# Where the outer rows of Wq are loaded from, and the row sizes of two sets of zero fills, in a decode step with its gradients

## The chip, the cores and the metric

One NeuronCore of a Trainium2 chip runs the whole kernel. The metric is device time in microseconds (us), the median of the runs shown. Engines are called as the profile calls them: PE (matmuls), DVE, ACT, POOL (GpSimd) and SP; the core has 16 DMA engines that all queues share.

## The reference

One token (batch 1, width 448) goes through an attention block with a sliding window over a key and value cache, and then through a bilinear feed-forward block. The outputs are the result and the gradients of x, both caches and all weights.

```python
def _A_ref(x, k_cache, v_cache, wq, wo):          # x normalised before
    W = 4096                                      # window of the 32768 positions
    q = heads(x @ wq)                             # 16 heads of 256
    k, v = last W positions of each cache, 8 kv heads, each for two q heads
    p = softmax(q k^T * Dh ** -0.5)
    return (p v) @ wo
h  = x + _A_ref(layernorm(x), ...)
h2 = h + ((n @ w_gate) * (n @ w_up)) @ w_down     # n = layernorm(h)
_out, _vjp = jax.vjp(f, x, k_cache, v_cache, wq, wo, w_gate, w_up, w_down)
return (_out, *_vjp(grad_out))
```

Only the last 4096 of 32768 positions of a cache get a gradient. The gradient of the other 28672 positions is zero, for 8 heads and two caches, and must be written all the same: 16 regions of 14 MB in `out_2` and `out_3`.

## The kernel before, in words

Wq (448 x 4096, 28 KB per partition when laid over 128 partitions) lives in the tile `zeros`, but not fully. Partitions 0 to 31 and 96 to 127 hold rows of Wq. In partitions 32 to 95 every fourth one (32, 36, ..., 92) is zeroed, 16 partitions in all, and is the source of the zero fills; the three between hold Wq rows. The Wq rows that the zero partitions displace are kept in part of the tile `Mt`, called `odd`.

The start, in the order of the code:

- L58 and L60: ACT's queue loads x and grad_out.
- L69: SP's queue loads Wq rows 0 to 31 in one DMA (32 partitions x 28 KB). L70: ACT's queue loads rows 96 to 127 in one DMA.
- L80 (`load_odd`, L76 to L78): SP's queue loads the displaced rows in four DMAs of 128 KB, packets of 4 KB.
- L81 to L86: DVE and ACT zero partitions 32 to 95 of `zeros` and parts of `odd`. DVE clears columns 0 to 8191 of partitions 32 to 63, then of 64 to 95 (L82), then the remaining columns of 32 to 63 (L83); ACT does the remaining columns of 64 to 95 (L84).
- L87 and L88: ACT's queue loads the Wq rows of partitions 33 to 95 that are not zero rows, three DMAs of 16 rows.
- L99 to L103: SP's queue gets the 15 full zero fills, each one region of 14 MB, 16 source partitions, in rows of 16 KB (`ZW`, 8192 elements), or of 28 KB (`NW`) for the regions in `LONG`. The first needs the memsets of L82.
- L116 to L118: SP's queue gets a part of the sixteenth region. `deal(eng, e0, k, n, f)` fills from `k` zero partitions starting with number `e0`, `n` rows of `f` elements from each; `deal_all` does it from all 16. The rest of that region is left to GpSimd, in two laps (`deal_rest`, L120 to L131): lap 0 after the output h2 (L566 to L568), lap 1 after the last gradients (L803 and L804).
- L178 to L183: GpSimd's queue loads the windows K0, V0, K1, V1 and V2 (2 MB each).

Then the forward pass runs over the 8 kv heads: scores, softmax, moments (`scores`, `softmax`, `moments`, L377 to L440), with GpSimd loading further windows as buffers come free (L460 to L470), then Wo, the feed-forward block and its gradients (to L595), then the gradient of the attention (from L597). In its last stage (L766 to L802) PE makes the outer products for the gradients of K and V, ACT and DVE copy them from PSUM to slots of the tile `BIG` (`evac`, L297), and GpSimd's queue writes a pair of slots per head (L801 and L802). In between GpSimd also writes the weights' gradients (`outer`, L644 to L652); the first of these (L715) write `out_7` from the slots that the gradients of the first head want next.

Each engine's instructions run in their program order, its DMAs too, and the scheduler adds semaphore waits. SP issues nothing but DMAs: its list of fills is a background stream that the DMA engines serve beside the loads and stores on GpSimd's queue. A zero fill's rows are written from the partitions given; `deal` thus sets how many bytes go from which zero partition.

```python
def fill(eng, flat, rows, n, f):
    p = len(range(128)[rows])
    eng.dma_start(out=flat.rearrange("(p n f) -> p n f", p=p, f=f), in_=zeros[rows, 0:f].unsqueeze(1).to_broadcast([p, n, f]))
```

Of the kernel before, what the change touches and what calls it, by code (L numbers as in the profile page):

```python
# [17 lines left out]
G = 8  # L18
# [9 lines left out]
HQ = H * Dh // 2  # L28
HF = F // 2
ZW = 8192  # L30
NW = NI * HQ
FL = (Sk - W) * Dh // 16

# [9 lines left out]
def kernel(  # L43
# [3 lines left out]
    V_, S_, P_ = nc.vector, nc.scalar, nc.tensor  # L47
    FILL = nc.sync
    IO = nc.gpsimd
# [12 lines left out]
    def flat_rows(w):  # L62
        return w.rearrange("a b -> (a b)").rearrange("(p x) -> p x", p=128)

    zeros = const.tile([128, NW], bf16)
    one = const.tile([128, 1], f32)
    V_.memset(one[:], 1.0)
    wq_rows = flat_rows(A_wq)
    FILL.dma_start(out=zeros[0:32, :], in_=wq_rows[0:32, :])  # L69
    S_.dma_start(out=zeros[96:128, :], in_=wq_rows[96:128, :])  # L70
    Mt = const.tile([128, G, 2, 2 * Dh], bf16)
    late = Mt[:].rearrange("p g f c -> p (g f c)")
    odd = late[:, 2 * HQ:4 * HQ]
    wq_odd = A_wq.rearrange("a b -> (a b)")[32 * NW:96 * NW].rearrange("(e h k c) -> e h k c", h=NI, k=4, c=HQ)

    def load_odd(eng):  # L76
        for k in range(4):
            eng.dma_start(out=odd[32 + k:96:4, :].rearrange("p (h c) -> p h c", h=2), in_=wq_odd[:, 0:2, k, :])  # L78

    load_odd(FILL)  # L80
    for p in (32, 64):  # L81
        V_.memset(zeros[p:p + 32, 0:ZW], 0.0)  # L82
    V_.memset(zeros[32:64, ZW:NW], 0.0)  # L83
    S_.activation(out=zeros[64:96, ZW:NW], in_=one[64:96, 0:1].to_broadcast([32, NW - ZW]), func=ACT.Copy, scale=0.0)  # L84
    for p in (0, 96):
# [4 lines left out]
    def region(o, g):  # L90
        return o[0, g, 0:Sk - W, :].rearrange("s d -> (s d)")
# [5 lines that stand above are left out]
    ALL = slice(32, 93, 4)  # L97
    LONG = range(5, 10)
    for g in range(G):  # L99
        for k, o in enumerate((out_2, out_3)):  # L100
            if (g, k) != (G - 1, 1):
                f = NW if 2 * g + k in LONG else ZW
                fill(FILL, region(o, g), ALL, FL // f, f)  # L103
    last = region(out_3, G - 1)
    used = [0]

    def deal(eng, e0, k, n, f=ZW):
        p0 = 32 + 4 * e0
        fill(eng, last[used[0]:used[0] + k * n * f], slice(p0, p0 + 4 * k - 3, 4), n, f)
        used[0] += k * n * f  # L110

    def deal_all(n, f):
        fill(FILL, last[used[0]:used[0] + 16 * n * f], ALL, n, f)
        used[0] += 16 * n * f

    deal(FILL, 0, 3, 14)  # L116
    deal_all(24, ZW)
    deal_all(8, 1224)  # L118

    def deal_rest(lap):  # L120
        if lap == 0:
            deal(IO, 0, 4, 24)
            deal(IO, 4, 3, 6)
            deal(IO, 7, 2, 38)
            deal(IO, 9, 7, 15)
        else:
            deal(IO, 0, 5, 2, 512)
            deal(IO, 5, 2, 25)
            deal(IO, 7, 2, 2, 512)
            deal(IO, 9, 7, 15)  # L130
            assert used[0] == 896 * ZW  # L131

# [423 lines left out]
    for n, (s, m0, m1) in enumerate(CH):  # L556
# [3 lines left out]
        for m in range(m0, m1):  # L560
            c = NI * s + m
# [5 lines left out]
    with tc.issue_after(h2_out.ins):  # L567
        deal_rest(0)  # L568
# [46 lines left out]
    for h in range(H):  # L615
        for dk in range(2):
            for hf in range(2):
                c0 = (h % 2) * Dh + dk * 128
                g = h // 2
# [150 lines left out]
    for s, g in enumerate(SEQ):  # L770
# [3 lines left out]
        for t in range(T):  # L774
            d_ps = bps.tile([128, 2, Dh], f32, tag="d2", bufs=4)
            k, a = t // 8, t % 8
# [26 lines left out]
    with tc.issue_after(tail.ins):  # L803
        deal_rest(1)  # L804
# [31 lines left out]
```

## Time and profile before

| what | value |
|---|---|
| median of 3 runs | 784.82 us (784.43 to 785.53) |
| the profiled execution | 784.74 us, of it 782.9 in the profile's span |
| PE, DVE, ACT, POOL busy | 60%, 52%, 21%, 5% of the span |
| bytes moved by DMA | 329.70 MB (SP's queue 228.94, GpSimd's 97.77) |
| HBM | 48.40 MB read, 280.59 MB written |
| first Wq DMA, SP (L69) | issued at 0.75, 896 KB, 6.9 us to landing |
| first Wq DMA, ACT (L70) | issued at 1.57, 896 KB, 13.0 us to landing |
| K0 (L157) | issued at 1.29, 2048 KB, 17.8 us to landing |
| lap 0 of GpSimd's fills | issued from 372.89, 1536, 288, 1216 and 1680 KB, landing 47.4, 54.1, 101.9 and 111.4 us after issue |
| last gradients' DMAs (L802), lap 1 | issued at 739.76 and 740.83 |

How to read it: the profile is one execution, its times count from the span's start. A view gives, for 40 equal slices or for stretches that one names, how busy each engine was, the mean busy share of the 16 DMA engines, and the GB/s that they moved. Another lists each queue's packets, MB and share of the DMA engines' time: q1 is SP's, q10 ACT's, q0 GpSimd's. A landing is counted from the issue, so it includes the time in the queue.

### The profile page before, as it was taken

To read this page: it belongs to the slowest core of one execution; us is meant where nothing else is said; L and a number is where in the kernel's file an instruction comes from. 1 tells how busy PE (TensorE), PEld (TensorE's weight loads), DVE (VectorE), ACT (ScalarE), POOL (GpSimd) and SP (SyncE) were. 2 spreads that over 40 slices of the span, in tenths; PEclk is the share of its full clock that TensorE was granted. 3 is DMA by queue.
4 is the path that set the end of the run, shared out by engine and by line. 5 is a ranking of instruction groups with operands and counts; after the bars stand their busy time and mean duration, and the time that the engine had idled before them with its cause. 6 is when DMAs were issued, how large, how long until landed. Compare 5 with 4: busy or idle time off the path is not lost.

```text
span 782.9 us, 11090 instructions
## 1 busy us (share of the span) xinstructions
PE 471.6 (60%) x4506; PEld 260.9 (33%) x4506; DVE 403.7 (52%) x1190; ACT 162.0 (21%) x270; POOL 42.3 (5%) x86
## 2 busy tenths in 40 slices
PE   0769999989897540303223377089978678862600
PEld 0656555555564220301113243034423233320300
DVE  7436776666676310202566543066656456589500
ACT  4022212211220000000210033044533334421300
POOL 2000000000000000000100100000000000000200
PEclk9999999999999765555555555555555555555555
DMA  9999999999999999999999999999999999999996
GB/s 285 425 427 425 427 429 426 427 428 424 432 424 425 438 426 434 432 433 434 427 426 437 426 423 420 431 430 433 429 425 429 429 433 428 428 431 429 430 431 270
DMA packets 23188, 329.70 MB, mean 421 GB/s; under 512 B 3149, under 2 KB 3151, under 8 KB 4486
## 3 DMA queue, kind: packets, MB, share of 16 engines
q1 hardware_dynamic: 12589, 228.94, 68.6%
q0 software_dynamic: 10400, 97.77, 29.8%
q10 hardware_dynamic: 148, 2.30, 0.9%
q8 instruction: 35, 0.57, 0.3%
q14 instruction: 16, 0.12, 0.0%
HBM read 48.40 MB, written 280.59 MB: 420 GB/s over the span
## 4 chain that ended last, share of the span: by engine, by line
PE 36%; DMA 31%; DVE 14%; issue 7%; ACT 4%; another core or an unknown queue 3%; POOL 1%; POOLq 0%; DVEq 0%; ACTq 0%
DMA BIG<-in_A_k_cache_dram 10%; DMA out_dram<-BIG 9%; DMA BIG<-in_B_w_down_dram 8%; PE d_ps L777 8%; PE tr L363 8%; PE MT L420 8%; ACT BIG L299 3%; DMA BIG<-in_A_wo_dram 3%; DVE BIG L602 3%; DVE BIG L663 2%; DMA BIG<-in_A_v_cache_dram 2%; DVE BIG L591 2%; DVE BIG L301 2%; PE dp L368 2%
## 5 line engine op out<-in xcount | busy, mean ns | idle before, releaser
L777 PE MATMUL d_ps<-BIG 32*128 32x512 bf16 x256 | 121.1, 599 | 65.1 <-ACT BIG L299 47.7
L420 PE MATMUL MT<-BIG 128*128 128x512 bf16 x512 | 142.2, 391 | 4.1 <-DMA BIG<-in_A_v_cache_dram 4.1
L416 DVE TENSOR_SCALAR BIG<-BIG,pf 128x256 bf16<-128x256 bf16 x512 | 111.6, 281 | 34.3 <-PE MT L420 32.1
L363 PE MATMUL tr<-ident_bf,BIG 128*128 128x128 bf16 x1024 | 113.3, 269 | 20.7 <-DVE doW L602 12.6
L299 ACT CAST BIG<-d_ps 128x512 bf16<-128x512 f32 x156 | 88.4, 587 | 180.2 <-PE d_ps L777 129.5
L363 PEld LDWEIGHTS <-BIG 128*128 128x128 bf16 x1024 | 81.6, 121 | 65.1 <-issue 57.0
L301 DVE COPY BIG<-tr 128x1024 bf16<-128x1024 bf16 x92 | 63.3, 688 | 53.2 <-PE tr L363 50.3
L301 DVE CAST BIG<-d_ps 128x512 bf16<-128x512 f32 x100 | 68.0, 684 | 39.4 <-DMA out_dram<-BIG 33.4
L299 ACT COPY BIG<-tr 128x1024 bf16<-128x1024 bf16 x36 | 36.4, 1012 | 130.6 <-PE tr L363 121.3
L368 PEld LDWEIGHTS <-BIG 128*128 128x128 bf16 x1024 | 37.0, 102 | 73.0 <-DVE BIG L301 44.8
L423 PEld LDWEIGHTS <-BIG 128*128 128x128 bf16 x512 | 42.5, 99 | 45.2 <-issue 9.0
L423 PE MATMUL acc<-pT_all,BIG 128*128 128x2 bf16 x512 | 45.0, 164 | 7.1 <-DVE kbar L440 6.2
L420 PEld LDWEIGHTS <-BIG 128*128 128x128 bf16 x512 | 38.5, 99 | 21.6 <-issue 5.9
L426 PE MATMUL acc<-pT_all,BIG 128*128 128x2 bf16 x512 | 44.2, 164 | 0.0
L777 PEld LDWEIGHTS <-BIG 32*128 32x128 bf16 x256 | 20.8, 111 | 70.3 <-issue 51.1
L541 DVE CUSTOM_DVE_ANT_0 dh_bc<-BIG,dh_bc 128x448 bf16<-128x448 bf16 x14 | 8.7, 624 | 57.6 <-DMA BIG<-in_B_w_down_dram 57.3
L426 PEld LDWEIGHTS <-BIG 128*128 128x128 bf16 x512 | 30.0, 96 | 0.9
L562 PE MATMUL y<-BIG,hh_bf 128*1 128x448 bf16 x14 | 5.9, 567 | 37.9 <-DMA BIG<-in_B_w_down_dram 37.2
L368 PE MATMUL dp<-doT,BIG 128*128 128x2 bf16 x512 | 24.2, 168 | 4.5 <-DVE BIG L301 3.7
L238 PE MATMUL t<-one,xe 1*128 1x1 f32 x42 | 11.2, 332 | 24.5 <-DVE xe L237 24.0
L368 PE MATMUL sT<-qT,BIG 128*128 128x2 bf16 x512 | 22.2, 165 | 2.6 <-issue 1.9
L758 DVE TENSOR_TENSOR BIG<-r_ps,mrow 96x1024 bf16<-96x1024 bf16 (+2 forms) x15 | 18.3, 1221 | 1.0 <-PE r_ps L763 0.8
(203 smaller groups left out, 382.1 us busy)
## 6 DMA issues: line engine op xcount, KB each, us to landing
out_dram<-zeros SPq DMA_DIRECT2D x15, 14336.0 KB, 168.2
out_dram<-BIG POOLq DMA_DIRECT2D x17, 2048.0 KB, 29.9
BIG<-in_A_v_cache_dram POOLq DMA_DIRECT2D x8, 2048.0 KB, 26.1
BIG<-in_A_k_cache_dram POOLq DMA_DIRECT2D x12, 1024.0 KB, 15.2
out_dram<-zeros SPq DMA_DIRECT2D x1, 6144.0 KB, 110.4
BIG<-in_A_k_cache_dram POOLq DMA_DIRECT2D x2, 2048.0 KB, 27.8
out_dram<-BIG POOLq DMA_DIRECT2D x2, 1792.0 KB, 27.5
out_dram<-zeros POOLq DMA_DIRECT2D x2, 1680.0 KB, 74.0
```

Of the source, the lines that this page charges most:

```text
L299: S_.copy(out=out, in_=in_)
L301: V_.tensor_copy(out=out, in_=in_)
L363: P_.transpose(tr[:, i, dh, :], x_at(g, 4 * q + i)[:, dh * 128:(dh + 1) * 128], ident_bf[:])
L368: P_.matmul(out_ps[:, 4 * q + i, :], lhsT=xt[:, i, dh, :], rhs=vecT[:, 4 * g + dh:4 * g + dh + 3:2], start=(dh == 0), stop=(dh == 1))
L416: V_.tensor_scalar(out=pk[:, i, h, :], in0=K[:, t, :], scalar1=pf[:, t, h:h + 1], scalar2=None, op0=ALU.mult)
L420: P_.matmul(MT[hf][:], lhsT=v_at(g, t)[:, hf * 128:(hf + 1) * 128], rhs=pk[:, i, :, :].rearrange("p h d -> p (h d)"), start=(t == 0), stop ...
L423: P_.matmul(acc[:, 2 * hf:2 * hf + 2], lhsT=v_at(g, t)[:, hf * 128:(hf + 1) * 128], rhs=pT_all[:, g, t, :], start=(t == 0 and hf == 0), st ...
L426: mm = P_.matmul(acc[:, 4 + dk:7 + dk:2], lhsT=K[:, t, dk * 128:(dk + 1) * 128], rhs=pT_all[:, g, t, :], start=False, stop=(t == T - 1), s ...
L591: V_.tensor_tensor_reduce(out=wv[:, i, :], in0=wv[:, i, :], in1=bc2[w][:, i % 2, :], scale=1.0, scalar=0.0, op0=ALU.mult, op1=ALU.add, acc ...
L602: V_.tensor_tensor_reduce(out=wg_sb[:, 0:D], in0=parked.get(b, wo_b(b)), in1=dh_bc[:], scale=1.0, scalar=0.0, op0=ALU.mult, op1=ALU.add, a ...
L758: V_.tensor_tensor(out=rows[p0:p1], in0=r_ps[p0:p1, :].unsqueeze(1).to_broadcast([p1 - p0, 8, 128]), in1=mrow[p0:p1, :].unsqueeze(2).to_br ...
L777: mm = P_.matmul(d_ps[:].rearrange("p w d -> p (w d)"), lhsT=rows[32 * k:32 * k + 32, a, :], rhs=R[32 * k:32 * k + 32, :], start=True, sto ...
```

## The change

The eight rows of each DMA, the split of the memsets and of the first fill, and the new pieces of lap 0 and lap 1:

```diff
+ZL = 12288
...
-    FILL.dma_start(out=zeros[0:32, :], in_=wq_rows[0:32, :])
-    S_.dma_start(out=zeros[96:128, :], in_=wq_rows[96:128, :])
+    for k in range(4):
+        for p in (0, 96):
+            IO.dma_start(out=zeros[p + k:p + 32:4, :], in_=wq_rows[p + k:p + 32:4, :])
...
-    for p in (32, 64):
-        V_.memset(zeros[p:p + 32, 0:ZW], 0.0)
+    for c in (0, ZW // 2):
+        for p in (32, 64):
+            V_.memset(zeros[p:p + 32, c:c + ZW // 2], 0.0)
...
-            if (g, k) != (G - 1, 1):
+            if g + k == 0:
+                first = region(o, g)
+                fill(FILL, first[0:FL * 16 // 7], ALL, 2 * FL // (7 * ZW), ZW // 2)
+                fill(FILL, first[FL * 16 // 7:], ALL, 6 * FL // (7 * ZW), ZW)
+            elif (g, k) != (G - 1, 1):
...
         if lap == 0:
-            deal(IO, 0, 4, 24)
-            deal(IO, 4, 3, 6)
-            deal(IO, 7, 2, 38)
-            deal(IO, 9, 7, 15)
+            deal(IO, 0, 4, 16, ZL)
+            deal(IO, 4, 3, 4, ZL)
+            deal(IO, 7, 2, 25, ZL)
+            deal(IO, 9, 7, 10, ZL)
         else:
             deal(IO, 0, 5, 2, 512)
             deal(IO, 5, 2, 25)
-            deal(IO, 7, 2, 2, 512)
+            deal(IO, 7, 2, 1, 5120)
             deal(IO, 9, 7, 15)
```

The 64 outer rows of Wq go to the head of GpSimd's queue, ahead of K0: eight DMAs, each of every fourth partition of one block of 32, blocks 0 and 96 in turn. SP's queue starts with the four `odd` DMAs, ACT's with x and grad_out as before. The first seventh of the first fill is written in rows of 8 KB (256 of them) from columns that the first two of the four halved memsets clear; the rest of it in 768 rows of 16 KB. In GpSimd's lap 0 the rows are 24 KB in place of 16 KB, with as many bytes per zero partition, but for numbers 7 and 8, where 8 KB each move from lap 0 to lap 1.

## The prediction

> **What bounds the kernel now.** I read the page's slices first. The DMA engines show 9 tenths or more in 39 of 40 slices, and the rate stands between 420 and 438 GB/s in all but the first and the last.
>
> ```profile
> DMA  9999999999999999999999999999999999999996
> GB/s 285 425 427 425 427 429 426 427 428 424 432 424 425 438 426 434 432 433 434 427 426 437 426 423 420 431 430 433 429 425 429 429 433 428 428 431 429 430 431 270
> DMA packets 23188, 329.70 MB, mean 421 GB/s; under 512 B 3149, under 2 KB 3151, under 8 KB 4486
> ```
>
> At the plateau, about 429 GB/s, 329.70 MB take 768.5 us; the span is 782.9. So only 14.4 us are not plain moving of bytes, and they must lie in the two end slices. The chain of waits names PE, DVE and loads, but the last compute is followed by a last pair of output DMAs at 739.76, and bytes move until about 778.4: compute is not the bound.
>
> Next the table by stretch, for the head and the tail. Its last two columns are DMA share and GB/s; a packet is booked where it starts, so a share can pass 1.
>
> ```profile
> 0.00:1.50 1.50, 0.00 (x0) 0.00 (x0) 0.06 (x1) 0.00 (x0) 0.41 (x5) 1.00 0.00 0
> 1.50:3.40 1.90, 0.00 (x0) 0.00 (x0) 1.61 (x1) 1.44 (x2) 1.90 (x4) 1.00 1.09 242
> 3.40:5.40 2.00, 0.00 (x0) 0.00 (x0) 1.86 (x1) 2.00 (x1) 1.99 (x10) 1.00 1.13 229
> 5.40:7.00 1.60, 0.00 (x0) 0.00 (x0) 0.85 (x1) 1.60 (x1) 0.93 (x3) 1.00 0.78 164
> 7.00:9.00 2.00, 0.00 (x0) 0.00 (x0) 2.00 (x1) 1.56 (x1) 0.00 (x0) 1.00 1.07 262
> 9.00:10.20 1.20, 0.00 (x0) 0.00 (x0) 0.62 (x1) 0.00 (x0) 0.00 (x0) 1.00 0.83 218
> 10.20:12.00 1.80, 0.00 (x0) 0.00 (x0) 1.69 (x1) 0.00 (x0) 0.00 (x0) 1.00 1.18 291
> 12.00:13.40 1.40, 0.00 (x0) 0.00 (x0) 0.93 (x1) 0.00 (x0) 0.00 (x0) 1.00 0.69 187
> 13.40:17.00 3.60, 0.00 (x0) 0.00 (x0) 3.12 (x2) 1.28 (x1) 0.00 (x0) 1.00 1.00 422
> ...
> 773.00:778.50 5.50, 0.00 (x0) 0.00 (x0) 0.00 (x0) 0.00 (x0) 0.00 (x0) 0.50 0.57 226
> 778.50:782.90 4.40, 0.00 (x0) 0.00 (x0) 0.00 (x0) 0.00 (x0) 0.00 (x0) 0.50 0.00 0
> ```
>
> From 1.5 to 13.4 the engines are busy (share about 1) but move half the plateau: 242x1.9 + 229x2.0 + 164x1.6 + ... = 2.75 MB, which at 429 GB/s is 6.4 us of work. Before 1.8 nothing moves. So the head loses 13.4 - 6.4 = 7.0 us, 5.2 of them in half-rate packets. The tail loses 5.5 x (1 - 226/429) = 2.6 us while engines run dry one by one, and 4.4 us of ending. 7.0 + 2.6 + 4.4 = 14.0, nearly all of the 14.4.
>
> Why half rate? The DMA view of two stretches answers, by ACT's queue q10 (packets, MB, share of 16 engines): first of 0 to 13.4 us, then of 16.5 to 19.5.
>
> ```profile
> q10 hardware_dynamic: 37, 0.92, 29.4%
> ```
>
> ```profile
> q10 hardware_dynamic: 48, 0.92, 71.2%
> ```
>
> Each holds 32 Wq rows of 28 KB. In the first (L70, partitions 96 to 127) they took 0.294 x 13.4 x 16 = 63 us, 1.97 each; in the second (L88, partitions spread over 33 to 95) 0.712 x 3 x 16 = 34 us, 1.07 each. Same tensor, row size and queue: what differs is that the slow rows all go to one block of 32 partitions. SP's rows into partitions 0 to 31 (L69) took 2.2 by the same sum.
>
> **The change, part by part.**
>
> *Wq rows by GpSimd.* The 64 outer rows leave SP and ACT and become eight DMAs of eight rows, every fourth partition, the blocks 0 and 96 in turn. If a DMA of eight rows runs on eight engines and the next takes the other eight, both blocks are written at once, each by half the engines. Then a row should cost 1.07, not 1.97 to 2.2, and the 4 rows per engine 4.3 us in place of 8.3. That k rows run on k engines I read from GpSimd's turn of fills issued at 372.9, pieces of 4, 3, 2 and 7 rows at a time, each 24, 6, 38 and 15 deep. The DMA view by stretch gives its queue 0.80 MB in 380 to 400 and 0.57 MB in 420 to 448, which is 2.5 and 1.25 rows of 16 KB per us; at 1.68 us for an engine's turn (below) that is 4.1 and 2.1 engines, the rows of the first and the third piece. In 404 to 414 it is 0.69 MB, 7.1 engines: more than any one of the first three, so they don't all sit on the same ones.
>
> The issue: small GpSimd DMAs take 0.51 each (L78 there: 2.04 for 4), the first DMA took 0.70; eight are about 4.3 us, from 1.29 to 5.6. That is one pair per 1.03 us, as fast as 16 engines eat it. How long from first issue to first bytes is not shown by itself. Lower end 1.0: SP issues at 0.75 and bytes move by 1.8. Upper end 4.5: K0's issue (L157) is at 1.29, and q0's first packets are in the stretch 5.4 to 7.0. I take 2.0, nearer the lower row, because two SP rows of 2.2 us stood on each engine before K0's and these are gone. So full rate from 3.3. Before that, SP's four `odd` DMAs (now its first; 0.6 us per issue, 131 KB each) move about 0.26 MB. By 13.4 us: 0.26 + 10.1 x 0.429 = 4.6 MB against 2.75: **4.3 us gained**. Ends: wait 1.0 gives 0.13 + 11.1 x 0.429 = 4.9 MB, 5.0 us; wait 4.5 gives 0.52 + 7.6 x 0.429 = 3.8 MB, 2.4 us.
>
> The Trainium skill, SBUF — State Buffer, section "Can I just issue two DMAs to hit both halves?", answers no: two DMAs at once, at partition 0 and at 64, measured 6% over one alone. That speaks against this part; with it the sum would be that of the first rival below. L69 and L70, one block each and queued together, did run at half rate here, which agrees; but each of them had rows on all 16 engines, and no row of this trace shows two DMAs on eight engines each.
>
> *What stands behind the eight on GpSimd's queue.* K0 to V2 (L178 to L183) are issued 4.3 us later, and the built order shows that K0 now waits for the semaphore of the first Wq DMA, V0 for that of the second, and so on: with first bytes at 5.8 and a row of 1.07 on top, K0 would wait until some 7 to 8. Behind them stand the identities (4.08 to 6.3 now), read by DVE at 31.4. K0 landed 17.8 us after its issue, with PE's first transposes at 32.1: covered. Were K0 later than that, it would delay compute, which has the 38 us below.
>
> *Memsets in halves.* L82's two memsets of 3.47 become four of 1.76 (L86's row for the same 32x2048), with two gaps more of 0.5 to 0.9: all is done about 1.5 us later (17.4 to about 19), and so is what DVE does next, ahead of the same cover. The first fill needs only the first two: 1.79 + 1.76 + 0.9 + 1.76 = 6.2 in place of 9.65. Its bytes follow at about 7.2, so SP covers any gap that K0's wait leaves. Of itself 0: between 7.2 and 13.4 GpSimd's queue feeds the engines anyway.
>
> *8 KB rows in a seventh of the first fill.* 2.1 MB in 256 packets for 128, 4.9 us of moving: 13.4 to 17 has smaller packets yet (4 KB, mixed in) and loses 2% (422 against 429), so 0 to 0.1 us. In taking turns with 16 KB rows it leaves K0 and V0 two thirds of the engines.
>
> *24 KB pieces in the turn (L122 to L125, at 372.9).* The engines take one packet of each queue in turn. A 16 KB row (0.61 us at 429/16 GB/s) beside SP's 28 KB row (1.07) is a turn of 1.68; with 24 KB (an estimate of 0.92) 1.99. The longest piece goes from 38 x 1.68 = 64 us to 25 x 1.99 = 50, the first from 40 to 32. So the turn drains some 15 to 25 us sooner, and the two out_7 blocks queued behind it too. For these the chain waits now:
>
> ```profile
> 482.18 0.57 ACT BIG L299
> 482.75 26.85 another core or an unknown queue
> 509.70 0.59 ACT BIG L299
> ```
>
> ACT may go on when they have been read out, so about 20 of the 26.85 go and compute ends near 720, not 740. Gain at the end: **0**, because the engines move the same bytes; SP's fills take what GpSimd leaves. Without this cover it would be worth up to 20. The bytes per engine are unchanged: 24, 6 and 15 rows are 16, 4 and 10 of 24 KB, and 38 rows with 2 KB are 25 with 10 KB. So the tail's 2.6 us stay, between 1.5 less and 1.0 more for another order at the end.
>
> **Sum.** The profiled execution took 784.74 (span 782.9 and 1.84 around it; the median is 784.82). 784.74 - 4.3 = 780.4, and with the median's 0.08 about **780.5**. What is late next is again the DMA engines, from 3.3 us on.
>
> **The rivals.**
>
> *The two halves don't run beside each other* (chance 0.14). Then the Wq rows flow at about 229 GB/s from 3.3 until SP's fill joins at 7.2, and full rate follows: 0.26 + 3.9 x 0.229 + 6.2 x 0.429 = 3.8 MB, a gain of 2.5: 782.2. For it: all rows of one block were slow now. Against: there all 16 engines wrote into one block at a time. By the skill's 6% it would be 243 in place of 229 for these 3.9 us, some 782.1.
>
> *All eight DMAs on the same eight engines* (slower; 0.09). If a DMA of 8 rows always starts at engine 0, half the engines get 8 rows each, not 4, and end 4 x 1.07 = 4.3 us later than the balance made by the other pieces. It decides where the head gains less than 4.3; with first bytes at 5.8 it gains 2.4, so 784.74 + 1.9 = 786.6. Against: the 7.1 engines of 404 to 414 above.
>
> *Same placing, early bytes, or a tail that eats the gain* (0.12): within 0.2% (1.6 us, about what a measurement can tell), around 784.5.
>
> **Chances.** Forecast 0.65 (779.7 to 782.3 by the wait alone), halves 0.14, no change 0.12, slower 0.09. Faster by over 0.2%: 0.79; same 0.12; slower 0.09. The range: 5.0 of head and 1.5 of tail give 778.2; upward it takes in the halves rival and 1.0 of tail and half of the no-change case: 784.0.
>
> **What would show it.** Right: the first slice rises from 285 to about 380 GB/s; in 3.3 to 13.4 share and rate agree at about 429; Wq rows at 1.07; the wait at 482 shrinks and the last output DMAs are issued near 720, with no gain from it. Wrong: shares near 1 at 230 GB/s until 7 (halves); a tail whose 226 GB/s stretch grows by 4 us (placing); first GpSimd bytes at 5.8.

## The result, and the profile after

The changed kernel takes 794.38 us (median of 4 runs, 793.78 to 794.76) against 784.62 of the kernel before (784.04 to 785.53): ratio 1.0123, 95% interval 1.0105 to 1.0140. It is 9.8 us slower; 4.3 us faster had been forecast. The profiled execution took 794.76, its span is 793.0.

The same slices as before, of the kernel after:

```profile
DMA  8999999999999999999999999999999999999992
GB/s 284 429 428 427 426 427 427 429 426 429 427 424 429 431 437 431 431 437 433 423 433 430 427 421 432 429 430 430 420 432 428 432 428 430 431 427 431 431 390 86
```

The middle is the plateau of 429 GB/s, as before. The first slice has 284 against 285: the head has gained nothing. The last two have 390 and 86 against 431 and 270: the whole loss is in the last 40 us. A table by stretch of the tail, of the kernel before and then of the one after (the last two columns are the busy share of the DMA engines and GB/s):

```profile
767.00:772.00 5.00, 0.00 (x0) 0.00 (x0) 0.00 (x0) 0.00 (x0) 0.00 (x0) 0.50 0.97 414
772.00:775.00 3.00, 0.00 (x0) 0.00 (x0) 0.00 (x0) 0.00 (x0) 0.00 (x0) 0.50 0.95 401
775.00:778.00 3.00, 0.00 (x0) 0.00 (x0) 0.00 (x0) 0.00 (x0) 0.00 (x0) 0.50 0.41 155
```

```profile
760.00:767.00 7.00, 0.00 (x0) 0.00 (x0) 0.00 (x0) 0.00 (x0) 0.00 (x0) 0.50 0.93 391
767.00:772.00 5.00, 0.00 (x0) 0.00 (x0) 0.00 (x0) 0.00 (x0) 0.00 (x0) 0.50 0.91 380
772.00:775.00 3.00, 0.00 (x0) 0.00 (x0) 0.00 (x0) 0.00 (x0) 0.00 (x0) 0.50 0.63 267
775.00:778.00 3.00, 0.00 (x0) 0.00 (x0) 0.00 (x0) 0.00 (x0) 0.00 (x0) 0.50 0.54 229
778.00:781.00 3.00, 0.00 (x0) 0.00 (x0) 0.00 (x0) 0.00 (x0) 0.00 (x0) 0.50 0.29 116
781.00:785.00 4.00, 0.00 (x0) 0.00 (x0) 0.00 (x0) 0.00 (x0) 0.00 (x0) 0.50 0.06 25
785.00:789.00 4.00, 0.00 (x0) 0.00 (x0) 0.00 (x0) 0.00 (x0) 0.00 (x0) 0.50 0.06 25
```

Shares times 16 are engines. Before, nearly all 16 work until 775 and stop together by 778. After, some 15 are left in 760 to 767 (in finer stretches 0.95 until 765, then 0.87, which is 14, until 770), some 9 between 775 and 778, and from 781 to 789 a share of 0.06: one single engine, which the kernel waits for. No byte was added (329.70 MB in both), so bytes have moved from some DMA engines to others.

The head after, in the stretches of the table in the prediction, and GpSimd's queue in the order of time:

```profile
3.40:5.40 2.00, 0.00 (x0) 0.00 (x0) 1.76 (x1) 2.00 (x1) 2.00 (x5) 1.00 0.57 207
5.40:7.00 1.60, 0.00 (x0) 0.00 (x0) 1.17 (x1) 1.60 (x1) 0.72 (x2) 1.00 0.70 228
```

```profile
1.31 4.23 POOL L72 DMA_DIRECT2D zeros<-in_A_wq_dram  x8 [0.85 <-POOLq L827]
5.53 0.59 POOL L164 DMA_DIRECT2D BIG<-in_A_k_cache_dram  x1
7.36 0.54 POOL L167 DMA_DIRECT2D BIG<-in_A_v_cache_dram  x1 [1.24 <-DMA zeros<-in_A_wq_dram]
8.77 0.53 POOL L167 DMA_DIRECT2D BIG<-in_A_k_cache_dram  x1 [0.87 <-DMA zeros<-in_A_wq_dram]
```

Before, the engines were busy (1.13) at 229 GB/s in 3.4 to 5.4. Now 0.57 are busy, at 207: the rate is as low, but mostly for another reason. The packets are less slow, and almost half the engines have nothing to do. The eight issues took 4.23 us as reckoned, and V0, K1 and the rest then waited for the Wq DMAs one by one and were issued 1.2 to 1.8 us apart. The packets in the trace show why: the rows of the eight DMAs start at 2.7, 4.5, 6.2, 7.4, 8.8, 10.6, 12.9 and 14.5 us, each set when the one before it is about through, and the last is through at 16.8. They went one after another, not in pairs.

Compute came close to what was forecast. ACT's stall, in the trace of before and then of after:

```profile
509.70 1.07 ACT L299 CAST BIG<-d_ps 128x512 bf16<-128x512 f32 x2 [26.95 <-DMA out_dram<-BIG]
```

```profile
493.61 1.07 ACT L306 CAST BIG<-d_ps 128x512 bf16<-128x512 f32 x2 [11.15 <-DMA out_dram<-BIG]
```

It is 15.8 us shorter, where about 20 were forecast. The last pair of outputs is issued at 723.44 in place of 739.76:

```profile
723.44 1.08 POOL L809 DMA_DIRECT2D out_dram<-BIG  x2 [5.53 <-issue]
```

### The profile page after: what moved, and what is told of

It reads as the page before. It is cut to its first block, busy times and chain, and to the rows that moved or that the text cites. A ratio compares the mean times of both kernels' runs of the same rounds, so it can differ in the third digit from the quotient of the medians.

```text
span 793.0 us, 11101 instructions
## 1 busy us (share of the span) xinstructions
PE 471.1 (59%) x4506; PEld 260.9 (33%) x4506; DVE 403.8 (51%) x1192; ACT 162.0 (20%) x270; POOL 46.3 (6%) x94
## 2 busy tenths in 40 slices
DMA packets 23043, 329.70 MB, mean 416 GB/s; under 512 B 2975, under 2 KB 2977, under 8 KB 4310
```

## The experiments

**The theory** (A, placing). GpSimd's plain two-dimensional DMAs (8x14336, 2x5120) of up to 16 rows put one row on each engine, from the first engine on; they don't move the place from which the next piece is dealt. Its three-dimensional pieces (96x1x8192 and so on) run on as many engines as they have source partitions and do move it. Two things follow. All eight Wq DMAs fall on engines 0 to 7: 8 rows of 28 KB each in place of 4, 4.3 us more than the mean, and 4.3 less on 8 to 15. And the 10 KB piece of lap 1 on zero partitions 7 and 8, now one row each, lost its third dimension, so the seven-row piece behind it is dealt from engine 7, not 9: 15 rows of 16 KB (9.2 us) too many for 7 and 8, and too few for 14 and 15. Added up: engine 7 is 13.5 us late, 0 to 6 are 4.3 late, 8 is 4.9, 9 to 13 are early by 4.3, 14 and 15 by 13.5. From ends of 775 to 778 that makes one engine near 790, eight near 780, five near 772, two near 763. The table above reads like that. But the trace names no engines (a number here is a place in the deal), so it had to be tried. **Rivals**: the order in which the 24 KB pieces are served (B), and the late K0 to V2 (C).

**x1: the shape alone, in the kernel before.** Same bytes and the same source rows.

```diff
-            deal(IO, 7, 2, 2, 512)
+            deal(IO, 7, 2, 1, 1024)
```

> The kernel before, with one number changed: the small piece of lap 1 on zero partitions 7 and 8 is one row of 2 KB each in place of two rows of 1 KB; the bytes stay the same, but the DMA's shape is 2x1024 in place of 4x1x512. Theory A (placing): GpSimd's plain two-dimensional DMAs put one row on each engine from the first on and don't move the place where the next piece starts; then the seven-row piece behind it, 15 rows of 16 KB (0.61 us each), lands two engines early, engines 7 and 8 get 15 rows too many (9.2 us) and 14 and 15 none. Engines end at 775 to 778 now, so one of them ends near 785 to 787 and the time is 791 to 794. Theory B (the turn): the loss of the changed kernel comes from the order in which 24 KB pieces, SP's fills and GpSimd's last pieces are served; this kernel has the old order, so 784.6, within 0.5.

Measured: 791.45 (before, on the same chip: 784.76), ratio 1.0095 (1.0079 to 1.0111). The tail:

```profile
778.00:781.00 3.00, 0.00 (x0) 0.00 (x0) 0.00 (x0) 0.00 (x0) 0.00 (x0) 0.50 0.13 55
781.00:785.00 4.00, 0.00 (x0) 0.00 (x0) 0.00 (x0) 0.00 (x0) 0.00 (x0) 0.50 0.10 41
```

0.13 of 16 is two engines, alone after 778: as many as the theory makes late here, 7 and 8. A piece of 4 KB that only drops a dimension costs 6.7 us.

**x2: that shape undone in the changed kernel.**

```diff
-            deal(IO, 7, 2, 1, 5120)
+            deal(IO, 7, 2, 5, 1024)
```

> The changed kernel, with the small piece of lap 1 as five rows of 2 KB (shape 10x1x1024) in place of one row of 10 KB (2x5120); same bytes. Theory A: the seven-row piece is back on its own engines; the last engine of 788.9 and the two that end near 760 go, but the eight Wq DMAs still sit on one half of the engines, which end 4.3 us late: last bytes near 780 to 781 in place of 788.9, time 785.5 to 787. Theory B: the order is unchanged, so about 794.4.

Measured: 786.53, ratio 1.0026 (1.0015 to 1.0037). 7.9 of the 9.8 us are gone.

```profile
775.00:778.00 3.00, 0.00 (x0) 0.00 (x0) 0.00 (x0) 0.00 (x0) 0.00 (x0) 0.50 0.50 212
778.00:781.00 3.00, 0.00 (x0) 0.00 (x0) 0.00 (x0) 0.00 (x0) 0.00 (x0) 0.50 0.20 74
781.00:785.00 4.00, 0.00 (x0) 0.00 (x0) 0.00 (x0) 0.00 (x0) 0.00 (x0) 0.50 0.00 0
```

The single engine has gone. What is left is a share of 0.50 in 775 to 778: as much as eight engines.

**x3: the new start with the old laps**, that is the changed kernel with the pieces of the kernel before.

```diff
-            deal(IO, 0, 4, 16, ZL)
-            deal(IO, 4, 3, 4, ZL)
-            deal(IO, 7, 2, 25, ZL)
-            deal(IO, 9, 7, 10, ZL)
+            deal(IO, 0, 4, 24)
+            deal(IO, 4, 3, 6)
+            deal(IO, 7, 2, 38)
+            deal(IO, 9, 7, 15)
...
-            deal(IO, 7, 2, 1, 5120)
+            deal(IO, 7, 2, 2, 512)
```

> The changed kernel's start (Wq rows by GpSimd in eight DMAs, halved memsets, 8 KB rows in the first fill) with the laps of the kernel before. Theory A: 8 rows of 28 KB on each of eight engines in place of 4 on all: those end 4 x 1.07 = 4.3 us after the others' balance, less what the head gained (under 1): 786 to 788.5. Theory B: no loss without the 24 KB pieces, 784.6 or up to 1 us less. Theory C (the head: K0 to V2 wait for the semaphores of the Wq DMAs and come late, and this lasts to the end): compute ends some 5 us later than before and the time follows it, 788 to 790, with engines ending together.

Measured: 787.64, ratio 1.0037 (1.0022 to 1.0051), again with a share of 0.50 in 775 to 778.

```profile
775.00:778.00 3.00, 0.00 (x0) 0.00 (x0) 0.00 (x0) 0.00 (x0) 0.00 (x0) 0.50 0.50 212
778.00:781.00 3.00, 0.00 (x0) 0.00 (x0) 0.00 (x0) 0.00 (x0) 0.00 (x0) 0.50 0.24 85
```

Its last outputs are issued at 738.17, no later than before's 739.76, so C falls.

**x4: the laps alone**, the 24 KB pieces in the kernel before, with the small piece in its harmless shape.

```diff
-            deal(IO, 0, 4, 24)
-            deal(IO, 4, 3, 6)
-            deal(IO, 7, 2, 38)
-            deal(IO, 9, 7, 15)
+            deal(IO, 0, 4, 16, 12288)
+            deal(IO, 4, 3, 4, 12288)
+            deal(IO, 7, 2, 25, 12288)
+            deal(IO, 9, 7, 10, 12288)
...
-            deal(IO, 7, 2, 2, 512)
+            deal(IO, 7, 2, 5, 1024)
```

> The kernel before with the 24 KB pieces of lap 0 and the 10 KB of lap 1 written as five rows of 2 KB (10x1x1024), nothing else changed. Theory A: same bytes on every engine, all engines busy to the end: 784.6 within 0.7, although compute ends 15 to 20 us earlier. Theory B: the order makes the loss: 789 to 794.

Measured: 783.51, ratio 0.9991 (0.9982 to 1.0001). No loss, so B falls. The last outputs are issued at 719.94, 20 us earlier than before, and the time gains about 1.

**z2: the same once more.**

> The same kernel as x4_laps_alone, for a closer interval: 783.0 to 784.0. If the 24 KB pieces are worth anything it must show at the end, since the head is the old one: all 16 engines busy until later (774 in place of 770 to 773) and a last byte before 777.5.

Measured: 783.67 against 784.72, ratio 0.9988 (0.9979 to 0.9997). The gain is small: the interval leaves out 1 here and just takes it in for x4. The two medians are the lowest of the study. The share in 767 to 772 is 0.99 (0.97 before), in 775 to 778 0.36 (0.41): the engines end closer together. Why the 24 KB pieces do that was not tried.

**y2: the Wq rows in four plain DMAs of 16 rows**, otherwise x2; GpSimd's queue keeps its order.

```diff
-    for k in range(4):
+    for k in range(2):
         for p in (0, 96):
-            IO.dma_start(out=zeros[p + k:p + 32:4, :], in_=wq_rows[p + k:p + 32:4, :])
+            IO.dma_start(out=zeros[p + k:p + 32:2, :], in_=wq_rows[p + k:p + 32:2, :])
```

> The changed kernel with the lap 1 piece in 10x1x1024 and the Wq rows in four plain DMAs of 16 rows (every second partition of a block of 32), blocks in turn. Theory A: 16 rows are one on each engine, so the bytes are balanced again and the 4.3 us go; all engines write into one block at a time, so rows cost about 2 us and the head gains nothing: 783 to 784.5. Rival (the loss of the eight Wq DMAs comes from their standing ahead of K0 on GpSimd's queue, not from the engines they run on): 786 to 787.5.

Measured: 783.99, ratio 0.9992 (0.9983 to 1.0002). Sixteen rows are one for each engine; the loss of x2 is gone though the rows stand as before ahead of K0. The DMA view, GpSimd's queue (packets, MB, share of 16 engines): first this kernel from 0 to 12 us, then the changed kernel from 4.4 to 5.0, which holds one of its eight-row DMAs.

```profile
q0 software_dynamic: 113, 1.84, 68.2%
```

```profile
q0 software_dynamic: 10, 0.23, 99.3%
```

64 rows took 0.682 x 12 x 16 = 131 us, 2.05 each, with 16 engines writing into one block of 32 partitions; 8 rows took 0.993 x 0.6 x 16 = 9.5 us, 1.19 each, with 8 engines. That DMA, the second, is one of the quicker ones. The first, from 2.4 to 3.0, took 1.303 x 0.6 x 16 = 12.5 us, 1.56 each, and the mean of all 64 rows, by their packets, is 1.33.

```profile
q0 software_dynamic: 22, 0.23, 130.3%
```

So rows are slow where many engines write into one block, as the prediction read it, though eight engines on one block are not always down to its 1.07. What failed in the main is which engines run.

**y3: the old Wq loads with all the rest of the change**, otherwise x2.

```diff
-    for k in range(4):
-        for p in (0, 96):
-            IO.dma_start(out=zeros[p + k:p + 32:4, :], in_=wq_rows[p + k:p + 32:4, :])
+    FILL.dma_start(out=zeros[0:32, :], in_=wq_rows[0:32, :])
+    S_.dma_start(out=zeros[96:128, :], in_=wq_rows[96:128, :])
```

> The changed kernel with the lap 1 piece in 10x1x1024 and the two Wq loads of the kernel before (SP and ACT): what is left of the change is the halved memsets, the 8 KB rows of the first fill and the 24 KB pieces. Theory A: no byte on another engine and the same head: as the laps alone, 783 to 784.3. Rival (8 KB rows or later memsets cost): 784.5 to 786.

Measured: 783.94, ratio 0.9992 (0.9982 to 1.0002), as x4. The halved memsets and the 8 KB rows cost and bring nothing that the time shows. The first slice of this kernel has 270 GB/s against 285, which is 0.29 MB or 0.7 us of moving less; what causes that was not looked for.

**y1 and z1: the Wq rows spread by their shape.** Each eight-row DMA of x2 is cut into two three-dimensional ones.

```diff
     for k in range(4):
-        for p in (0, 96):
-            IO.dma_start(out=zeros[p + k:p + 32:4, :], in_=wq_rows[p + k:p + 32:4, :])
+        for i in range(2):
+            for p in (0, 96):
+                zv = zeros[p + k:p + 32:4, :].rearrange("q (i c) -> q i c", c=HQ)
+                wv = wq_rows[p + k:p + 32:4, :].rearrange("q (i c) -> q i c", c=HQ)
+                IO.dma_start(out=zv[:, i::2, :], in_=wv[:, i::2, :])
```

> The changed kernel with the lap 1 piece in 10x1x1024, and each Wq DMA of eight rows cut into two three-dimensional ones (8x4x2048 and 8x3x2048: every second 4 KB block of a row), blocks 0 and 96 still in turn; 16 DMAs. Theory A: three-dimensional pieces of eight rows go to eight engines from a place that moves on, so the two blocks of partitions are served by the two halves of the engines side by side and all 16 get the same bytes. The 4.3 us of imbalance go, and the head gains what the prediction looked for, less the longer issue (16 x 0.53 = 8.5 us): by 13.4 us some 4.1 MB in place of 2.75, 3 us: 780 to 781.5. Rival (two DMAs never run beside each other on the two blocks, whatever their shape): engines balanced but no gain in the head, 783 to 784.5. Rival (the place doesn't move for loads): as with the old shape, 786.5.

> The same kernel as y1_spread_by_shape, for an ordinary profile and a closer time (the profile there was of an execution 3 us above its median). If the head's gain of about 1 us survives, 783.0 to 783.6 and engines that end a microsecond earlier than with the old loads; if it is eaten at the end, 784 and one or more engines ending after the rest.

Measured: 784.32, ratio 0.9997 (0.9987 to 1.0006), and again 783.94, ratio 0.9990 (0.9981 to 0.9999). Two of the ten executions of y1 took 786.83 and 787.55, the second of them the profiled one, so the profile of z1 is read here. Its head:

```profile
3.40:5.40 2.00, 0.00 (x0) 0.00 (x0) 1.76 (x1) 2.00 (x1) 2.00 (x5) 1.00 0.96 328
```

Engines busy (0.96) and 328 GB/s, where the changed kernel had 0.57 and 207. The first slice has 314 GB/s against 285: 29 x 19.6 us = 0.57 MB, 1.3 us of moving. That is the kind of gain the change was expected to bring, a third of its size; GpSimd's 16 issues end only at 11.1, which may be why it is no more. The time is no better than that of x4, which has the old head. The microsecond does reach the tail: the shares in 772 to 775 and 775 to 778 are 0.81 and 0.15, against 0.92 and 0.36 in z2, so the engines end about 1 us earlier on average. But the last byte moves at 777.2 against 777.5, and the span is 782.0 against 781.5. Why the last engine and the ending do not follow the average was not found.

**z3: the fills moved to meet the Wq rows.** As x2, but 7 rows of 16 KB per engine go from engines 0 to 7 to engines 8 to 15.

```diff
-    deal_all(24, ZW)
+    deal_all(16, ZW)
...
             deal(IO, 9, 7, 10, ZL)
+            deal(IO, 0, 8, 2, 4096)
+            deal(IO, 8, 8, 10, ZL)
```

> The changed kernel with the lap 1 piece in 10x1x1024, eight Wq DMAs on one half of the engines as they are, and the fills moved to meet it: SP's last piece on all 16 goes from 24 to 16 rows, and GpSimd's lap 0 gets 1 row of 16 KB for each of engines 0 to 7 and 15 for each of 8 to 15 (as 24 KB and 8 KB rows). That takes 7 rows, 4.3 us, from engines 0 to 7 and gives them to 8 to 15. Theory A: engines end together again, 782.5 to 784.5. If the eight late engines weren't 0 to 7: they end 8.6 us apart, 790 or more. Rival (it's the place on GpSimd's queue that costs): 786.5 or above.

Measured: 784.38, ratio 0.9995 (0.9986 to 1.0004).

```profile
775.00:778.00 3.00, 0.00 (x0) 0.00 (x0) 0.00 (x0) 0.00 (x0) 0.00 (x0) 0.50 0.39 147
778.00:781.00 3.00, 0.00 (x0) 0.00 (x0) 0.00 (x0) 0.00 (x0) 0.00 (x0) 0.50 0.00 0
```

The eight Wq DMAs are untouched, and of the 2.9 us by which x2 is slower than the mean of x4 and z2 all but 0.8 are gone: the late engines were the first eight of the deal, by about the amount reckoned.

**z4: y1 with its two inner loops exchanged**, so that the even and odd halves of one set of rows follow each other.

```diff
-        for i in range(2):
-            for p in (0, 96):
+        for p in (0, 96):
+            for i in range(2):
```

> The kernel y1_spread_by_shape with its loops exchanged: the two DMAs of a set of eight rows (even and odd 4 KB blocks) follow each other, so the two halves of the engines write into the same block of 32 partitions at a time. Even blocks are 4 and odd ones 3, so one half of the engines has 16 KB (0.6 us) more than the mean. Theory A with a limit per block of partitions: 4 KB packets of these DMAs take about 0.3 us in place of 0.16, the first slice falls from 313 back to about 285 GB/s, 784.5 to 786. Without such a limit: as y1 in the head, 313 GB/s, and 784 to 785.

Measured: 787.89, ratio 1.0034 (1.0017 to 1.0051), but not for the reason given: the first slice has 318 GB/s, so the head as a whole lost nothing. The issues come 0.57 us apart (ten in 5.74 us) with 98 to 131 KB each, some 200 GB/s, which is less than the 229 that one block took in the kernel before; so most of this head could not show the limit. One stretch shows it, GpSimd's queue from 5.8 to 7.2, when issued pieces had piled up. First z1, then this kernel:

```profile
q0 software_dynamic: 236, 0.36, 84.8%
```

```profile
q0 software_dynamic: 182, 0.30, 80.6%
```

That is 257 GB/s with the two blocks in turn and 214 with one block at a time, each from one execution. The loss in time is in the tail, where one to two engines are busy after 778:

```profile
778.00:781.00 3.00, 0.00 (x0) 0.00 (x0) 0.00 (x0) 0.00 (x0) 0.00 (x0) 0.50 0.10 37
```

The last outputs were issued at 737.56, 13 us later than in z1. That alone does not make engines late: z3 issues them at 737.91 and the kernel before at 739.76, with shares of 0.00 and 0.01 after 778. The profiled execution of y1 (787.55) has the same tail (0.09 after 778), with its last outputs issued at 730.33. What makes the two engines late stays open.

## Why the prediction was wrong

Two steps failed, for one reason. The first is "If a DMA of eight rows runs on eight engines and the next takes the other eight", with the evidence "That k rows run on k engines I read from GpSimd's turn of fills". The reading of the fills was right. But they are three-dimensional pieces, and the Wq DMAs are not; x2, y2 and z3 show that the plain ones all go to the same eight. The second is "The bytes per engine are unchanged", which counted the 10 KB piece and not its shape.

The Trainium skill, DMA: Bandwidth & Descriptors, section "Why a DMA increments its semaphore by 16 and not by 1", has both rules: from GpSimd k consecutive engines from a moving cursor where k is below 16, and for some direct copies k = 16, with the partitions divided by 16, rounded up, on each engine. The runs agree (7.9 us in x2, 6.7 in x1), and show what is such a copy here: 8x14336 and 2x5120 are, 8x4x2048 and 50x1x12288 are not.

Point by point:

- *What bounds the kernel*: right. All of the change's effect is in the head and the tail.
- *4.3 us gained in the head*: wrong, 0 (first slice 284 against 285). The wait to the first bytes was within its ends, 1.4 us by the packets where 2.0 was taken; the rate was not, with half the engines without Wq rows.
- *Rows at 1.07*: too low, 1.33 on average (1.19 and 1.56 in the stretches above). That a block of partitions limits the rows is right (2.05 in y2, with 16 engines on one block). But quicker rows do not help when only eight engines have them.
- *The rival "all eight DMAs on the same eight engines"*: this is what happened, with a chance of 0.09. Its price of 4.3 us for the late engines came to 2.5 to 3.0 in the time (x2 against x4 and y2, with eight engines in 775 to 778). That its 786.6 is so near to x2's 786.53 is luck: it took off 2.4 us for a head that gained nothing, and put the 24 KB pieces, which gave 1.1, at 0. The evidence against it, 7.1 engines in 404 to 414, was the same wrong transfer from the fills.
- *"The bytes per engine are unchanged"*: wrong, and the largest term. The shape of the 10 KB piece moved the piece behind it, 7.9 us (x2), 6.7 in the kernel before (x1). No case of the prediction had it. Either of the two losses alone would have put the time above the range's 784.0 (786.53 in x2, 791.45 in x1).
- *24 KB pieces: the turn 15 to 25 us sooner, compute out near 720, at the end 0, within 1.5 less and 1.0 more*: right. The two longest pieces landed 77.2 and 89.2 us after their issue in place of 101.9 and 111.4; the last outputs were issued at 723.44, with 15.8 us in place of about 20 off the stall; and x4 and z2 took 1.1 us less.
- *Memsets and 8 KB rows at 0*: right in the time (y3).
- *The rival by which two DMAs never run beside each other on two blocks*, with the 6% of the Trainium skill, SBUF — State Buffer, section "Can I just issue two DMAs to hit both halves?": in the changed kernel they didn't, since both were on the same engines. In z1, on different engines by their shape, 328 GB/s flow in 3.4 to 5.4, SP's loads included, against 207. GpSimd's queue alone moves 257 GB/s in 5.8 to 7.2, 20% above the 214 of z4, which has one block at a time. So by these two profiles the two blocks are served side by side when the engines differ, and by more than the 6%; how far it goes these runs do not show, since the issues bound them.

Added up from the runs: 784.7, less 1.1 for the 24 KB pieces, plus 2.9 for eight Wq DMAs on half the engines (x2 less the mean of x4 and z2), plus 7.9 for the moved piece: 794.4. These terms are differences from run to run, so they must add up to the time measured. What bears them out is that the last two were found again in other surroundings: 2.9 in x3 and 6.7 in x1, each against the kernel before.

## What to carry to other kernels

Where the DMA engines are the bound, as here, the engine with the most bytes left sets the end: add up bytes per engine, not in all, for every DMA with fewer than 16 rows. An edit that leaves bytes and rows the same but lets two dimensions merge can change which engines a DMA runs on, and that of the ones dealt after it. In a profile it shows as a busy share at the end that stands at a multiple of 1/16 (0.50, 0.13 and 0.06 here), with the middle unchanged.

## What the runs showed of the hardware that was not expected

- From GpSimd, 2x1024 in place of 4x1x512, both 4 KB, made the kernel 6.7 us slower; two engines were left over at the end, as when the DMA behind it runs two engines early.
- Eight plain DMAs of eight rows, issued 0.53 us apart into two different blocks of partitions in turn, began to move 1.2 to 2.3 us apart, while a share of 0.43 of the engines was idle (3.4 to 5.4).
- 28 KB rows took 2.05 us with 16 engines on one block of 32 partitions, 1.33 on average with eight, and 1.07 spread over more partitions.
